# Sums of experts 1 to 6 turned back by VectorE and a scratch in memory, weight loads three chunks further ahead, gathers two experts ahead of use

## The chip, the core and the metric

The kernel runs on one core of one Trainium2 chip. The metric is the device time of one execution in microseconds (us). Engines have the names of the profile: PE is TensorE, DVE is VectorE, ACT is ScalarE, POOL is GpSimd, SP is SyncE, which here only issues DMAs.

## The reference

Retention (attention with a decay in place of the softmax) over 8 sequences of 576 tokens and 8 heads makes a row of 512 features for each of 4608 tokens. A mixture of experts follows: a token whose skip score is positive goes to one of 8 experts, and the expert's output, times its gate weight, is added to the row.

```python
ret = scores * Dmat[None, :, :, :]
x = np.matmul(ret, v).transpose(0, 2, 1, 3).reshape(B * S, H * D)      # 4608 x 512
do_compute = x @ w_skip > 0
e_idx = np.argmax(xc @ w_gate, axis=1)                                  # xc = x[do_compute]
for e in range(E):
    h = np.maximum(xc[mask] @ w1[e], 0.0)                               # 512 -> 1024
    y[mask] = gate_w[mask, None] * (h @ w2[e])                          # 1024 -> 512
out[do_compute] = xc + y
```

## The kernel before, in words

The first 160 us compute the retention, write every row to `out` in memory and rank the tokens by expert. The change lies in the rest, the experts. They are numbered 0 to 7 here, as in the code (the words "experts two to seven" count from one and mean 1 to 6), and taken in falling order of their counts. Expert e holds CAPS[e] = 368, 344, 332, 308, 304, 286, 278, 276 slots: two full blocks of 128, and a rest of 20 to 112, which is packed with the rests of other experts into a third block.

**Steps.** The 1024 hidden features are 8 chunks of 128. In step (e, f) PE computes `up` of chunk f (12 matmuls into `ph`, three for each of the four parts of the 512 inputs), then `down` of the chunk before it (12 matmuls which add to four PSUM banks `py_0` to `py_3`, each 128 output features by all slots of the expert, three matmuls a bank, one bank after the other). So the last `down` of expert e, of chunk 7, stands between `up` of chunks 0 and 1 of expert e+1, and the first `down` of expert e+1, which overwrites the four banks, stands behind `up` of chunk 1. Of the two halves of a step's place in the program, place 0 lies behind its `up`, place 1 behind its `down`.

**Precision.** Every f32 operand is split into a high part and a low rest. Of the weights ACT writes `whi` and DVE writes `wlo` from the loaded chunk `w` (4 buffers; 6 of each half). Of the hidden values ACT writes `hhi` (with the ReLU) and DVE `hlo` (lines 457 and 458), both before `down` of that chunk can run.

**Way in and out.** POOL gathers an expert's rows from `out` (`xg`, indirect DMA). SP writes them to a scratch in memory and reads them back in four pieces, a DVE transpose of 32 by 32 blocks (line 1026) turns them, ACT and DVE split them (`xhi`, `xlo`). For the way out `evacuate` copies the four banks to `yT` and `yR` (the rest), alternating ACT and DVE by bank; in the next expert's steps 1 and 2 PE turns each of the two blocks by four transposes (line 1000) and DVE's line 980 makes `rs` = gate times sum plus the old row, which POOL scatters to `out`. Expert 0 is computed with tokens on the partitions and needs no turn.

**Order.** PE runs its instructions in the order of the code. On the other engines a scheduler lays out each queue when the program is built, by its own estimate of when operands are ready; the chip then runs each queue as it was laid out. The call `split_raw` asks for the splits of the chunks that were loaded, five chunks ahead of their use (`AHEAD`).

Of the kernel before, what the change touches and what calls it, by code (L numbers as in the profile page):

```python
# [23 lines left out]
P = 128  # L24
# [9 lines left out]
NBLK = 3  # L34
# [16 lines left out]
AHEAD = 5  # L51
GROUPS = (8, 8, 8, 4, 4, 4)
# [31 lines left out]
def kernel(  # L84
# [90 lines left out]
    def by_chunk(x):  # L175
        return x.rearrange("t (p c) -> t c p", c=NCC)

# [755 lines left out]
    def down(e, f, ks, py, h, w):  # L933
        if e == 0:
            w2 = [p[:, 1].rearrange("p c i -> p (c i)") for p in w]
            for k, n in ks:
                three(py[k][:n], [([p[:, k * P : k * P + n] for p in h], w2)], f == 0, f == NFC - 1)
        else:
            m = CAPS[e]
            for c in range(NCC):  # L940
                three(py[c][:, :m], [([p[:, 1, c, :] for p in w], [p[:, :m] for p in h])], f == 0, f == NFC - 1)
# [5 lines left out]
    def evacuate(e, py):  # L947
        if e == 0:
            return py
        (q, at), n = PLACE[e], CAPS[e] - FULL  # L950
        if q not in yR:
            yR[q] = mp.tile([P, NCC, P], F32, tag="yR", name=f"yR_{q}")
            if at:
                nc.gpsimd.memset(yR[q][:, :, :at], 0.0)
        rest = yR[q]
        if e == NE - 1:
            rest = yR[e] = mp.tile([P, NCC, n], F32, tag="yE", name=f"yR_{e}", bufs=1)
        yT = mp.tile([P, NCC, FULL], F32, tag="yT", name=f"yT_{e}", bufs=1)
        copies = [nc.scalar.copy, nc.vector.tensor_copy]
        for c in range(NCC):  # L960
            copies[c % 2](yT[:, c, :], py[c][:, :FULL])
            if e < NE - 1:
                copies[c % 2](rest[:, c, at : at + n], py[c][:, FULL : FULL + n])
        if e == NE - 1:
            for c in range(NCC):
                nc.scalar.copy(rest[:, c, :], py[c][:, FULL : FULL + n])
        return yT

    def finish_rest(y, n, xr, scale, idx, tag):
        yn = bank(tag, f"yn_{y.name}", 2 if tag == "ph" else 1)  # L970
        for c in range(NCC):
            nc.tensor.transpose(yn[:n, c * P : (c + 1) * P], y[:, c, :n], ident)
        put(yn, n, scale[:n], xr[:n], idx[:n], f"rs_{y.name}")
# [19 lines left out]
    def finish(e, y, xg, ks, tags=("pt", "m")):  # L993
        for k, n in ks:
            if e == 0:
                yn = y[k]
            else:
                yn = bank(tags[k % len(tags)], f"yn_{e}_{k}", 2 if tags[k % len(tags)] == "ph" else 1)
                for c in range(NCC):
                    nc.tensor.transpose(yn[:n, c * P : (c + 1) * P], y[:, c, k * P : k * P + n], ident)  # L1000
# [22 lines left out]

    def turn_pieces(name):
# [6 lines left out]
    def gather_next(e, xg):  # L1031

        xg[e] = mp.tile([P, NBLK - 1, DM], F32, tag="xg", name=f"xg_{e}", bufs=3)
# [27 lines left out]
    def experts(acts):  # L1061
# [43 lines left out]
        at(NE - 1, 4, 0, lambda: tc.keep_in_program_order(nc.gpsimd.drain()))  # L1105
        for e in range(2, NE):
            at(e - 1, 0, 0, lambda e=e: gather_next(e, xg))
# [3 lines left out]
            for k, (name, rows) in enumerate(hops):  # L1111
                at(e - 1, 2 + k // 2, k % 2, lambda name=name, rows=rows: hop_out(name, rows()))
                at(e - 1, 3 + k // 2, k % 2, lambda name=name: hop_in(name))
        for n in range(len(steps) + 1):
# [3 lines left out]
            if cur:  # L1118
                e, f, ks = cur
                i = chunks.index((e, f))  # L1120
                for c in chunks[i : i + AHEAD + 1]:
                    if c not in wq and c not in raw and c[0] < len(regs):
                        raw[c] = load_w(*c, regs)
                if ks is not late and n > 3:
                    split_raw(1 if i == NCUT else len(raw))
# [27 lines left out]
            elif last:  # L1153
# [9 lines left out]
                if f == NFC - 1:  # L1163
                    y = evacuate(e, py[e])
                    if e + 1 < NE:
                        ks = blocks(e)[:-1] if e else blocks(e)
                        for k, where in zip(ks, ((1, 1), (2, 0), (2, 1))):
                            at(e + 1, *where, finish, e, y, xg[e], [k])
# [142 lines left out]
```

## Time and profile before

| | us |
|---|---|
| three runs | 404.70, 404.83, 405.85 (median 404.83) |
| profiled execution, its own time | 407.06 |
| its span (first to last instruction) | 405.4 |
| PE busy, share of the span | 380.5, 94% |
| DVE busy | 279.8, 69% |
| ACT busy | 184.0, 45% |
| mean granted clock of PE, of full speed | 0.992 |

The profiled execution has 1.7 us around its span and lies 2.2 us above the median of the three runs. Expert 1's first `up` starts at 199.73 us, and the last matmul of expert 7 at 396.16 us. A busy PE is not PE at its peak, since its matmuls overlap and their ends are modelled; the distance between two starts is what a matmul takes of PE's time. On DVE and ACT, too, an instruction may start some hundredths before the one ahead of it ends.

### The profile page before, as it was taken

To read this page: it belongs to the slowest core of one execution; us is meant where nothing else is said; L and a number is where in the kernel's file an instruction comes from. 1 tells how busy PE (TensorE), PEld (TensorE's weight loads), DVE (VectorE), ACT (ScalarE), POOL (GpSimd) and SP (SyncE) were. 2 spreads that over 40 slices of the span, in tenths; PEclk is the share of its full clock that TensorE was granted. 3 is DMA by queue.
4 is the path that set the end of the run, shared out by engine and by line. 5 is a ranking of instruction groups with operands and counts; after the bars stand their busy time and mean duration, and the time that the engine had idled before them with its cause. 6 is when DMAs were issued, how large, how long until landed. Compare 5 with 4: busy or idle time off the path is not lost. (4 is left out here: it accounts for less than half of the span.)

```text
span 405.4 us, 12478 instructions
## 1 busy us (share of the span) xinstructions
PE 380.5 (94%) x4950; PEld 345.4 (85%) x4952; DVE 279.8 (69%) x623; ACT 184.0 (45%) x367; POOL 154.1 (38%) x210
## 2 busy tenths in 40 slices
PE   7899989989999887999999999999999999999992
PEld 3677777778787775979899999999999999999992
DVE  3665686588589788977756766797768567777512
ACT  2454544445444566115544543545535546455311
POOL 4965654565475489051032024023042032200402
PEclk9999999999999899999999999999999999999998
DMA  8998999999999986236987666776776776673101
GB/s 304 352 331 306 352 303 350 321 335 308 331 348 325 352 327 185 81 86 224 311 261 251 202 203 212 235 254 233 244 218 238 227 243 226 233 259 107 66 2 56
DMA packets 39420, 99.34 MB, mean 245 GB/s; under 512 B 5678, under 2 KB 12974, under 8 KB 39358
## 3 DMA queue, kind: packets, MB, share of 16 engines
q1 hardware_dynamic: 30366, 78.66, 57.5%
q0 software_dynamic: 3232, 9.99, 7.2%
q10 hardware_dynamic: 5760, 9.85, 6.5%
q8 instruction: 40, 0.66, 0.7%
q14 instruction: 22, 0.18, 0.1%
HBM read 80.63 MB, written 18.26 MB: 244 GB/s over the span
## 5 line engine op out<-in xcount | busy, mean ns | idle before, releaser
L168 DVE TENSOR_TENSOR wlo_w<-w,whi_w 128x1024 fp32r<-128x1024 f32 x59 | 71.9, 1224 | 38.3 <-ACT whi_w L167 37.7
L167 ACT CAST whi_w<-w 128x1024 fp32r<-128x1024 f32 x59 | 61.7, 1051 | 52.2 <-PE py L449 48.6
L981 POOL DMA_INDIRECT out<-rs,sidx x17 | 21.5, 1264 | 126.3 <-DVE rs L980 118.1
L449 PE MATMUL ph<-xhi,whi_w 128*128 128x344 f32 (+6 forms) x224 | 68.4, 305 | 0.0
L449 PE MATMUL py<-hhi,whi_w 128*128 128x344 f32 (+6 forms) x224 | 68.2, 304 | 0.0
L449 PE MATMUL py<-hhi,wlo_w 128*128 128x344 f32 (+6 forms) x224 | 67.7, 302 | 0.0
L449 PE MATMUL ph<-xlo,whi_w 128*128 128x344 f32 (+6 forms) x224 | 67.7, 302 | 0.0
L449 PE MATMUL ph<-xhi,wlo_w 128*128 128x344 f32 (+6 forms) x224 | 67.7, 302 | 0.0
L449 PE MATMUL py<-hlo,whi_w 128*128 128x344 f32 (+6 forms) x224 | 67.6, 302 | 0.0
L588 POOL TENSOR_TENSOR kn<-u,tt_sb 128x512 f32<-128x512 f32 x33 | 35.0, 1060 | 46.6 <-DMA u<-qkv 19.4
L457 ACT ACTIVATE hhi<-ph 128x344 fp32r<-128x344 f32 (+8 forms) x61 | 26.0, 426 | 57.3 <-PE ph L449 57.2
L580 ACT COPY u<-psc 64x256 f32<-64x256 f32 x64 | 23.4, 366 | 58.5 <-DVE u L576 52.5
L670 PE MATMUL pxt<-u,vs 128*64 128x128 f32 (+1 forms) x576 | 49.0, 273 | 0.1
L607 POOL TENSOR_TENSOR vs<-u,tt_sb 64x256 f32<-64x256 f32 x72 | 44.8, 622 | 9.5 <-PE pxt L670 4.4
L576 DVE TENSOR_TENSOR u<-psc,mt_sb 64x256 f32<-64x256 f32 x72 | 30.3, 420 | 23.5 <-PE pxt L646 10.5
L621 PEld LDWEIGHTS ps_s<-u,kn 128*64 128x64 f32 x512 | 31.8, 139 | 12.8 <-issue 5.9
L449 PEld LDWEIGHTS ph<-xhi,whi_w 128*128 128x128 f32 x224 | 42.2, 189 | 0.1
L449 PEld LDWEIGHTS ph<-xlo,whi_w 128*128 128x128 f32 x224 | 42.2, 188 | 0.1
L449 PEld LDWEIGHTS py<-hhi,whi_w 128*128 128x128 f32 x224 | 42.2, 189 | 0.0
L449 PEld LDWEIGHTS py<-hlo,whi_w 128*128 128x128 f32 x224 | 42.2, 188 | 0.0
L449 PEld LDWEIGHTS py<-hhi,wlo_w 128*128 128x128 f32 x224 | 42.2, 188 | 0.0
L449 PEld LDWEIGHTS ph<-xhi,wlo_w 128*128 128x128 f32 x224 | 42.2, 188 | 0.0
(216 smaller groups left out, 825.0 us busy)
## 6 DMA issues: line engine op xcount, KB each, us to landing
u<-qkv SPq DMA_DIRECT2D x72, 512.0 KB, 5.9
w<-w SPq DMA_DIRECT2D x64, 512.0 KB, 4.6
out<-xn ACTq DMA_DIRECT2D x36, 256.0 KB, 5.9
hop<-xg SPq DMA_DIRECT2D x12, 256.0 KB, 4.7
xh<-hop SPq DMA_DIRECT2D x48, 64.0 KB, 2.7
hop_r<-xr SPq DMA_DIRECT2D x2, 256.0 KB, 2.7
xh_r<-hop_r SPq DMA_DIRECT2D x8, 64.0 KB, 5.0
out<-rs,sidx POOLq DMA_INDIRECT x17, 5.8
```

Source lines behind the costliest of these rows:

```text
L167: nc.scalar.copy(hi, t)
L168: nc.vector.tensor_tensor(lo, t, hi.bitcast(F32), ALU.subtract)
L449: nc.tensor.matmul(ps, x, y, start=first and n == 0, stop=last and n == 3 * len(terms) - 1)
L457: nc.scalar.activation(hi, ph, AF.Relu)
L576: nc.vector.tensor_tensor(u_t[g][h, j, :, :D], near[h, :, :D], mt_sb[h].unsqueeze(1).broadcast_to([D, NPR, D]), ALU.mult)
L580: nc.scalar.copy(u_t[g][h, j, :, D:], near[h, :, D:])
L588: nc.gpsimd.tensor_tensor(kn_t[g].rearrange("p a (j i) -> p a j i", j=2), u_t[g][:, 3].rearrange("p a (j i) -> p a j i", j=2), tt_sb[:, k ...
L607: nc.gpsimd.tensor_tensor(vs_t[g][h, j], u_t[g][h, 2, :, j * D : (j + 1) * D], tt_sb[h, TV + g % NQ // 2, :].unsqueeze(2).broadcast_to([D, ...
L621: nc.tensor.matmul(ps_s[halves[j], i % 2, a, :], kn_t[g][:, a, j * D : (j + 1) * D], u_t[g][:, 2, a, j * D : (j + 1) * D], start=i == 0 an ...
L670: nc.tensor.matmul(pxt[halves[j], a, q], vs_t[g][:, j, a, :], u_t[g][:, j, a, q], start=False, stop=a == NPR - 1, skip_group_check=True,)
L981: done = nc.gpsimd.indirect_dma_start(out=out, out_offset=bass.IndirectOffsetOnAxis(ap=idx, axis=0), in_=rs[:n], in_offset=None, bounds_ch ...
```

## The change

For experts 1 to 6 PE's transposes of the two full blocks go. `evacuate` lets DVE transpose each of the four banks in 32 by 32 blocks out of PSUM (`yp`), and leaves all copies of the rest, `yR`, to ACT. `pieces_out` writes `yp` to a scratch in memory in four DMAs of 128 KB (runs of 512 bytes), `rows_in` reads it back as rows (`yr`, one DMA of 512 KB), and `finish` takes `yr` in place of PE's result, in step 4 of the next expert. So that the pieces of 32 features lie right, the columns of `w2` are stored in another order, expert 0's `down` reads them in runs of 32, and the transposes that are left (line 981 of the new kernel) write in runs of 32.

From expert 1 on, loads of weights are issued up to 8 chunks ahead, with the same 4 buffers; the splits stay 5 ahead, and at an expert's first step (from expert 2 on) they are asked for behind the evacuation. Gathers are issued an expert earlier, with a fourth buffer of `xg`, and the hops of the gathered rows two steps earlier; POOL's drain moves from step 4 to step 6 of expert 7.

```diff
@@ -49,6 +49,7 @@
 UAHEAD = UBUFS - LAG
 VBUFS = 3
 AHEAD = 5
+LEAD = 3
 GROUPS = (8, 8, 8, 4, 4, 4)
 KONE = 2
 QD = 32
@@ -174,6 +175,9 @@
 
     def by_chunk(x):
         return x.rearrange("t (p c) -> t c p", c=NCC)
+
+    def by_piece(x):
+        return x.rearrange("t (p c i) -> t c p i", p=NQD, i=QD)
 
     def route_a(t0, n):
 
@@ -932,9 +936,10 @@
 
     def down(e, f, ks, py, h, w):
         if e == 0:
-            w2 = [p[:, 1].rearrange("p c i -> p (c i)") for p in w]
+            w2 = [p[:, 1].rearrange("f c (p i) -> f p c i", i=QD) for p in w]
             for k, n in ks:
-                three(py[k][:n], [([p[:, k * P : k * P + n] for p in h], w2)], f == 0, f == NFC - 1)
+                to = py[k][:n].rearrange("t (p c i) -> t p c i", p=NQD, i=QD)
+                three(to, [([p[:, k * P : k * P + n] for p in h], w2)], f == 0, f == NFC - 1)
         else:
             m = CAPS[e]
             for c in range(NCC):
@@ -955,12 +960,16 @@
         rest = yR[q]
         if e == NE - 1:
             rest = yR[e] = mp.tile([P, NCC, n], F32, tag="yE", name=f"yR_{e}", bufs=1)
+        if e < NE - 1:
+            yp = mp.tile([P, FULL // QD, NCC, QD], F32, tag="yp", name=f"yp_{e}", bufs=1)
+            for c in range(NCC):
+                marks["evacuated"] = nc.vector.transpose(yp[:, :, c, :], py[c][:, :FULL].rearrange("p (j t) -> p j t", t=QD))
+                nc.scalar.copy(rest[:, c, at : at + n], py[c][:, FULL : FULL + n])
+            return yp
         yT = mp.tile([P, NCC, FULL], F32, tag="yT", name=f"yT_{e}", bufs=1)
         copies = [nc.scalar.copy, nc.vector.tensor_copy]
         for c in range(NCC):
             copies[c % 2](yT[:, c, :], py[c][:, :FULL])
-            if e < NE - 1:
-                copies[c % 2](rest[:, c, at : at + n], py[c][:, FULL : FULL + n])
         if e == NE - 1:
             for c in range(NCC):
                 nc.scalar.copy(rest[:, c, :], py[c][:, FULL : FULL + n])
@@ -969,7 +978,7 @@
     def finish_rest(y, n, xr, scale, idx, tag):
         yn = bank(tag, f"yn_{y.name}", 2 if tag == "ph" else 1)
         for c in range(NCC):
-            nc.tensor.transpose(yn[:n, c * P : (c + 1) * P], y[:, c, :n], ident)
+            nc.tensor.transpose(by_piece(yn[:n])[:, c], y[:, c, :n], ident)
         put(yn, n, scale[:n], xr[:n], idx[:n], f"rs_{y.name}")
 
     def finish_pack(q):
@@ -992,12 +1001,12 @@
 
     def finish(e, y, xg, ks, tags=("pt", "m")):
         for k, n in ks:
-            if e == 0:
-                yn = y[k]
+            if e == 0 or e in yr:
+                yn = yr[e][:, k, :] if e else y[k]
             else:
                 yn = bank(tags[k % len(tags)], f"yn_{e}_{k}", 2 if tags[k % len(tags)] == "ph" else 1)
                 for c in range(NCC):
-                    nc.tensor.transpose(yn[:n, c * P : (c + 1) * P], y[:, c, k * P : k * P + n], ident)
+                    nc.tensor.transpose(by_piece(yn[:n])[:, c], y[:, c, k * P : k * P + n], ident)
             put(yn, n, gate[:n, k, e : e + 1], xg[:n, k, :], sidx[:n, k, e : e + 1], f"rs_{e}_{k}")
 
     xr, xrT, xh, hop = {}, {}, {}, {}
@@ -1020,6 +1029,20 @@
         rows = hop.pop(name).rearrange("(h t) (p c) -> p t h c", t=QD, c=P)
         for p in range(NQD):
             nc.sync.dma_start(xh[name][p * QD : (p + 1) * QD], rows[p])
+
+    def pieces_out(e, yp):
+        with tc.issue_after(marks["load"].ins):
+            hop[e] = dram.tile([FULL, DM], F32, tag="hopy", name=f"hopy_{e}")
+            rows = hop[e].rearrange("(j t) (p c) -> p t j c", t=QD, c=P)
+            for p in range(NQD):
+                nc.sync.dma_start(rows[p], yp[p * QD : (p + 1) * QD].rearrange("t j c i -> t j (c i)"))
+
+    def rows_in(e):
+        with tc.issue_after(marks["load"].ins):
+            yr[e] = mp.tile([P, FULL // P, DM], F32, tag="yr", name=f"yr_{e}", bufs=1)
+            nc.sync.dma_start(yr[e], hop.pop(e).rearrange("(k t) c -> t k c", t=P))
+
+    yr = {}
 
     def turn_pieces(name):
         xt = mp.tile([P, NCC, P], F32, tag="xt", name=f"xt_{name}")
@@ -1030,7 +1053,7 @@
 
     def gather_next(e, xg):
 
-        xg[e] = mp.tile([P, NBLK - 1, DM], F32, tag="xg", name=f"xg_{e}", bufs=3)
+        xg[e] = mp.tile([P, NBLK - 1, DM], F32, tag="xg", name=f"xg_{e}", bufs=4)
         gather(e, xg[e], blocks(e)[:-1])
         q = PLACE[e][0]
         if q not in xr:
@@ -1102,15 +1125,16 @@
         at(2, 7, 1, count_more)
         at(0, 6, 0, pack_move)
         at(0, 7, 1, lambda: behind("up", pack_ids))
-        at(NE - 1, 4, 0, lambda: tc.keep_in_program_order(nc.gpsimd.drain()))
+        at(NE - 1, 6, 0, lambda: tc.keep_in_program_order(nc.gpsimd.drain()))
         for e in range(2, NE):
-            at(e - 1, 0, 0, lambda e=e: gather_next(e, xg))
+            at(*{2: (1, 0), 3: (1, 5)}.get(e, (e - 2, 0)), 0, lambda e=e: gather_next(e, xg))
             hops = [(f"{e}_{k}", lambda e=e, k=k: xg[e][:, k, :]) for k in range(NBLK - 1)]
             if e == PACKS[PLACE[e][0]][0]:
                 hops.append((f"r{PLACE[e][0]}", lambda e=e: xr[PLACE[e][0]]))
             for k, (name, rows) in enumerate(hops):
-                at(e - 1, 2 + k // 2, k % 2, lambda name=name, rows=rows: hop_out(name, rows()))
-                at(e - 1, 3 + k // 2, k % 2, lambda name=name: hop_in(name))
+                n = (e - 1) * NFC - 2 * (e > 3) + k // 2
+                at(*divmod(n, NFC), k % 2, lambda name=name, rows=rows: hop_out(name, rows()))
+                at(*divmod(n + 1, NFC), k % 2, lambda name=name: hop_in(name))
         for n in range(len(steps) + 1):
             cur = steps[n] if n < len(steps) else None
             if n in acts:
@@ -1118,11 +1142,12 @@
             if cur:
                 e, f, ks = cur
                 i = chunks.index((e, f))
-                for c in chunks[i : i + AHEAD + 1]:
+                for c in chunks[i : i + AHEAD + 1 + (LEAD if e else 0)]:
                     if c not in wq and c not in raw and c[0] < len(regs):
                         raw[c] = load_w(*c, regs)
-                if ks is not late and n > 3:
-                    split_raw(1 if i == NCUT else len(raw))
+                due = sum(c in chunks[: i + AHEAD + 1] for c in raw)
+                if ks is not late and n > 3 and (f or e < 2):
+                    split_raw(1 if i == NCUT else due)
                 if (e, f) not in hs:
                     tg, nb = (f"_{f}", 1) if e == 0 and f < NCUT else ("", 3)
                     hs[e, f] = [
@@ -1162,10 +1187,17 @@
                 down(e, f, ks, py[e], hs[e, f], wq[e, f])
                 if f == NFC - 1:
                     y = evacuate(e, py[e])
+                    if 0 < e < NE - 1:
+                        with tc.issue_after(marks["evacuated"].ins):
+                            split_raw(due)
                     if e + 1 < NE:
-                        ks = blocks(e)[:-1] if e else blocks(e)
-                        for k, where in zip(ks, ((1, 1), (2, 0), (2, 1))):
-                            at(e + 1, *where, finish, e, y, xg[e], [k])
+                        if e:
+                            at(e + 1, 0, 1, pieces_out, e, y)
+                            at(e + 1, 2, 0, rows_in, e)
+                            at(e + 1, 4, 1, lambda e=e: behind("up", finish, e, None, xg[e], blocks(e)[:-1]))
+                        else:
+                            for k, where in zip(blocks(e), ((1, 1), (2, 0), (2, 1))):
+                                at(e + 1, *where, finish, e, y, xg[e], [k])
                         if e and PACKS[PLACE[e][0]][-1] == e:
                             at(e + 1, 2, 1, finish_pack, PLACE[e][0])
                     else:
@@ -1292,7 +1324,9 @@
     wg = np.zeros((P, NCC, WP), f)
     wg[:, :, :NW] = w9
     w1 = moe_w1.reshape(NE, NCC, P, NFC, P).transpose(0, 3, 2, 1, 4).reshape(NE, NFC, P, DM)
-    w2 = moe_w2.reshape(NE, NFC, P, NCC, P).swapaxes(3, 4).reshape(NE, NFC, P, DM)
+    place = np.arange(DM).reshape(P, NCC).T.ravel()
+    there = np.argsort(place)[np.arange(DM).reshape(NQD, NCC, QD).swapaxes(0, 1).ravel()]
+    w2 = moe_w2.reshape(NE, NFC, P, DM)[..., there]
     w = np.ascontiguousarray(np.concatenate([w1, w2], axis=3))
     ins = {"qkv": qkv, "mtab": mtab, "gtab": gtab, "ttab": ttab, "wg": wg, "w": w}
```

The following shows where DVE's and ACT's queues differ. DVE at the boundary from expert 6 to expert 7, before; `hlo_0` and `hlo_1` are of expert 7's chunks 0 and 1, `py_` of expert 6, `wlo_w_5` of a chunk of expert 7.

```order
L168 TENSOR_TENSOR wlo_w_4_5830_5833<-w_4_5830,whi_w_4_5830_5832 128x1024
L458 SCALAR_TENSOR_TENSOR hlo_0_5872<-ph_0_0_5873,hhi_0_5871 128x276
L961 COPY yT_5900<-py_1_5594 128x256
L963 COPY yR_5213<-py_1_5594 128x22
L961 COPY yT_5900<-py_3_5596 128x256
L963 COPY yR_5213<-py_3_5596 128x22
L168 TENSOR_TENSOR wlo_w_5_5865_5868<-w_5_5865,whi_w_5_5865_5867 128x1024
L458 SCALAR_TENSOR_TENSOR hlo_1_5916<-ph_1_0_5917,hhi_1_5915 128x276
```

The same place of the changed kernel; `rs` and `yr` are of expert 5, the `wlo` of chunks 1 to 4 of expert 7.

```order
L169 TENSOR_TENSOR wlo_w_1_5583_5699<-w_1_5583,whi_w_1_5583_5698 128x1024
L462 SCALAR_TENSOR_TENSOR hlo_0_5857<-ph_0_0_5858,hhi_0_5856 128x276
L966 STREAM_TRANSPOSE yp_5885<-py_0_5606 128x8x32
L169 TENSOR_TENSOR wlo_w_2_5622_5748<-w_2_5622,whi_w_2_5622_5747 128x1024
L989 SCALAR_TENSOR_TENSOR rs_0_5735<-yr_5645,both,xg_4509 128x512
L989 SCALAR_TENSOR_TENSOR rs_1_5740<-yr_5645,both,xg_4509 128x512
L966 STREAM_TRANSPOSE yp_5885<-py_1_5607 128x8x32
L966 STREAM_TRANSPOSE yp_5885<-py_2_5608 128x8x32
L169 TENSOR_TENSOR wlo_w_3_5659_5787<-w_3_5659,whi_w_3_5659_5786 128x1024
L966 STREAM_TRANSPOSE yp_5885<-py_3_5609 128x8x32
L169 TENSOR_TENSOR wlo_w_4_5696_5824<-w_4_5696,whi_w_4_5696_5823 128x1024
L462 SCALAR_TENSOR_TENSOR hlo_1_5908<-ph_1_0_5909,hhi_1_5907 128x276
```

Between `hlo_0` and `hlo_1` stood two copies of 256 columns, two of 22 and one weight split; now four transposes, three weight splits and two `rs` stand there, and the last bank is read behind all but one of them.

DVE at the boundary from expert 5 to expert 6 of the changed kernel (`rs` of expert 4; the queue before had the pattern of the first piece above).

```order
L966 STREAM_TRANSPOSE yp_5565<-py_0_5270 128x8x32
L169 TENSOR_TENSOR wlo_w_2_5286_5412<-w_2_5286,whi_w_2_5286_5411 128x1024
L989 SCALAR_TENSOR_TENSOR rs_0_5399<-yr_5309,both,xg_4091 128x512
L989 SCALAR_TENSOR_TENSOR rs_1_5404<-yr_5309,both,xg_4091 128x512
L462 SCALAR_TENSOR_TENSOR hlo_0_5537<-ph_0_0_5538,hhi_0_5536 128x278
L966 STREAM_TRANSPOSE yp_5565<-py_1_5271 128x8x32
L169 TENSOR_TENSOR wlo_w_3_5323_5451<-w_3_5323,whi_w_3_5323_5450 128x1024
L966 STREAM_TRANSPOSE yp_5565<-py_2_5272 128x8x32
L169 TENSOR_TENSOR wlo_w_4_5360_5492<-w_4_5360,whi_w_4_5360_5491 128x1024
L966 STREAM_TRANSPOSE yp_5565<-py_3_5273 128x8x32
L169 TENSOR_TENSOR wlo_w_5_5409_5575<-w_5_5409,whi_w_5_5409_5574 128x1024
L462 SCALAR_TENSOR_TENSOR hlo_1_5590<-ph_1_0_5591,hhi_1_5589 128x278
```

Here the first transpose, a split and both `rs` even stand ahead of `hlo_0`, and the other three transposes have a split between each two.

ACT at the same boundary, before and then now.

```order
L457 ACTIVATE hhi_0_5525<-ph_0_0_5527 128x278
L961 COPY yT_5561<-py_0_5247 128x256
L963 COPY yR_5213<-py_0_5247 128x30
L961 COPY yT_5561<-py_2_5249 128x256
L167 CAST whi_w_5_5519_5521<-w_5_5519 128x1024
L963 COPY yR_5213<-py_2_5249 128x30
L457 ACTIVATE hhi_1_5576<-ph_1_0_5578 128x278
```

```order
L461 ACTIVATE hhi_0_5536<-ph_0_0_5538 128x278
L967 COPY yR_5227<-py_0_5270 128x30
L168 CAST whi_w_3_5323_5450<-w_3_5323 128x1024
L461 ACTIVATE hhi_1_5589<-ph_1_0_5591 128x278
L967 COPY yR_5227<-py_1_5271 128x30
L168 CAST whi_w_4_5360_5491<-w_4_5360 128x1024
L967 COPY yR_5227<-py_2_5272 128x30
L168 CAST whi_w_5_5409_5574<-w_5_5409 128x1024
L967 COPY yR_5227<-py_3_5273 128x30
```

The four `yR` copies, which with the transposes set the banks free, now lie one behind each of three weight casts, three of them behind `hhi_1`, which itself waits for `up` of chunk 1.

## Rows read from the trace of the kernel before

**Rows 1.** Waits of PE from 170 us on (total, times, longest).
```profile
PE py L449 <- DVE hlo L458: 0.7, 1, 0.7
```

**Rows 2.** Length, busy us of PE, PEld, DVE, ACT, POOL; clock; DMA share.
```profile
337.00:364.00 27.00, 27.00 (x211) 27.00 (x210) 19.48 (x29) 14.70 (x24) 2.91 (x3) 1.00 0.69 232
```

**Rows 3.** PE's turns back of sums (min/median/max ns, first, last start).
```profile
L1000 PE MATMUL yn<-ident,yT x56: 270/272/329, 237.5 to 397.5; 128*128 128x128 f32 x56
```

**Rows 4.** Timeline of PE around one turn (start us, us, instruction, count).
```profile
349.52 0.30 PE L449 MATMUL py<-hhi,wlo_w 128*128 128x278 f32 x1
349.65 0.60 PE L1000 MATMUL yn<-ident,yT 128*128 128x128 f32 x4
350.01 0.37 PE L449 MATMUL ph<-xhi,whi_w 128*128 128x278 f32 x1
350.22 0.29 PE L449 MATMUL ph<-xlo,whi_w 128*128 128x278 f32 x1
```

**Rows 5.** DVE by line, 227 to 400 us (busy us, mean ns | idle).
```profile
L168 DVE TENSOR_TENSOR wlo_w<-w,whi_w 128x1024 fp32r<-128x1024 f32 x45 | 55.1, 1224 | 29.3 <-ACT whi_w L167 28.7 <-PE ph L449 0.3
...
L1026 DVE STREAM_TRANSPOSE xt<-xh 128x512 f32<-128x512 f32 x10 | 11.0, 1101 | 0.0
L980 DVE SCALAR_TENSOR_TENSOR rs<-yn,both,xg 128x512 f32<-128x512 f32 x14 | 10.4, 747 | 5.7 <-PE yn L1000 5.6
L173 DVE TENSOR_TENSOR xlo<-xt,xhi 128x512 fp32r<-128x512 f32 x10 | 6.8, 685 | 0.7 <-ACT xhi L172 0.7
L961 DVE COPY yT<-py 128x256 f32<-128x256 f32 x14 | 5.9, 421 | 2.9 <-PE py L449 2.8
```

**Rows 6.** ACT by line, the same stretch.
```profile
L167 ACT CAST whi_w<-w 128x1024 fp32r<-128x1024 f32 x45 | 47.3, 1051 | 42.6 <-PE py L449 41.5 <-DMA xh<-hop 1.1
...
L963 ACT COPY yR<-py 128x88 f32<-128x88 f32 (+5 forms) x12 | 2.5, 208 | 0.0
```

**Rows 7.** Timeline of PE, boundary from expert 5 to 6.
```profile
345.24 0.30 PE L449 MATMUL py<-hhi,wlo_w 128*128 128x286 f32 x1
...
348.10 0.29 PE L449 MATMUL py<-hhi,whi_w 128*128 128x278 f32 x1
...
349.27 0.29 PE L449 MATMUL py<-hhi,whi_w 128*128 128x278 f32 x1
```

**Rows 8.** Timeline of DVE, the same boundary.
```profile
345.71 0.44 DVE L458 SCALAR_TENSOR_TENSOR hlo<-ph,hhi 128x278 fp32r<-128x278 f32 x1
346.07 0.42 DVE L961 COPY yT<-py 128x256 f32<-128x256 f32 x1
```

**Rows 9.** Timeline of ACT, the same boundary.
```profile
346.64 1.05 ACT L167 CAST whi_w<-w 128x1024 fp32r<-128x1024 f32 x1
347.60 0.18 ACT L963 COPY yR<-py 128x30 f32<-128x30 f32 x1
```

**Rows 10.** Timeline of ACT, boundary from expert 6 to 7.
```profile
370.90 0.40 ACT L457 ACTIVATE hhi<-ph 128x276 fp32r<-128x276 f32 x1 [0.67 <-PE ph L449]
```

**Rows 11.** Timeline of PE, the same boundary.
```profile
374.85 0.29 PE L449 MATMUL py<-hhi,whi_w 128*128 128x276 f32 x1
```

**Rows 12.** Timeline of ACT, boundary from expert 3 to 4.
```profile
287.87 0.29 ACT L172 CAST xhi<-xt_r 128x120 fp32r<-128x120 f32 x1
```

**Rows 13.** Timeline of PE, the same boundary.
```profile
294.84 0.30 PE L449 MATMUL py<-hhi,whi_w 128*128 128x304 f32 x1
```

**Rows 14.** Timeline of ACT, boundary from expert 4 to 5.
```profile
315.94 0.26 ACT L172 CAST xhi<-xt_r 128x88 fp32r<-128x88 f32 x1
```

**Rows 15.** Timeline of PE, the same boundary.
```profile
322.67 0.29 PE L449 MATMUL py<-hhi,whi_w 128*128 128x286 f32 x1
```

**Rows 16.** Timeline of ACT at the end of expert 7.
```profile
396.95 0.17 ACT L966 COPY yR<-py 128x20 f32<-128x20 f32 x1 [0.31 <-DVE yT L961]
```

**Rows 17.** DMA issues (count, KB each, median us to landing).
```profile
w<-w SPq DMA_DIRECT2D x64, 512.0 KB, 4.6
```

**Rows 18.** PE by line, 170 to 210 us: transposes that read every fourth element.
```profile
L930 PE MATMUL pt<-ident,xg 128*128 128x128 f32 x12 | 2.2, 279 | 0.0
```

## The prediction

> **What bounds the kernel now.** I read the waits of PE from the first expert on, then the busy time of all engines in windows of one expert, then the timeline of PE, DVE and ACT at each boundary between two experts. The first says that PE waits for nothing worth a name in 236 us: its largest entry is one wait of 0.7 us [rows 1]. The second says the same from the other side: over an expert PE is busy 27.00 of 27.00 us at a granted clock of 1.00, while DVE is busy 19.48 and ACT 14.70 [rows 2]. So in the stretch that the change touches, time goes only with work that leaves PE's queue, and comes only with waits that enter it. DVE and ACT have about a quarter and a half of each expert idle, but an idle share is no promise for the few us at a boundary, and there the timelines have to be followed instruction by instruction.
>
> **What PE loses.** PE turns sums by 56 transposes, four to a block [rows 3]. Of the 14 blocks, the 12 of experts 1 to 6 go, the two of expert 7 stay. A group of four starts at 349.65, just behind a matmul that started at 349.52, and the second matmul behind it starts at 350.22 [rows 4]; the rows between show the group and one more matmul. From 349.65 to 350.22 are 0.57 us, less the 0.13 us that one matmul takes (349.52 to 349.65): 0.44, say 0.43 us. 12 x 0.43 = 5.2 us go.
>
> **What the boundary asks for.** Behind the last `down` of an expert PE has `up` of the next expert's chunk 1 and then its first `down`, which overwrites the four banks. Bank c is needed three matmuls after bank c-1: at the boundary from 5 to 6 the last `down` of expert 5 starts at 345.24, the first of expert 6 at 348.10, and bank 3 is needed at 349.27 [rows 7]. Before, DVE had 0.42 us of copy for a bank and started on them at 346.07, right behind `hlo_0` [rows 8]. Now each bank needs a transpose on DVE and then the `yR` copy on ACT; where both read one bank, ACT's copy starts behind DVE's read [rows 16]. The queues run in order: the `yR` copy at 347.60 reads a bank that was full since 345.5 and starts only when the weight cast ahead of it is over [rows 9]. So what stands between the transposes in the new queues is on the path, however early its operands were ready.
>
> **Prices.** A transpose of 256 columns out of PSUM isn't in this trace. Half of the 512-column transpose from SBUF, which takes 1.10 us, is 0.55; a copy of the same bank takes 0.42 [rows 5], the lower bound; the upper is 0.62, if the transpose has a fixed part of 0.15 us (1.10 less 0.15, halved, plus 0.15; the fixed part is an estimate from the copy of 30 columns, which takes 0.18 [rows 9]). I take 0.55, since it comes from the same instruction. `rs` took 0.75 with one operand in PSUM; now all three lie in SBUF, and the nearest row is `xlo` with 0.69; `wlo` takes 1.22 [rows 5]. Starts on DVE follow about 0.08 closer than the durations (345.71 + 0.44 against 346.07 [rows 8]), so a queue advances by 0.47 for a transpose, 0.61 for `rs`, 1.15 for `wlo`, 0.36 for `hlo`.
>
> [...]
>
> **Boundary 5 to 6.** The order of DVE shown above: the last `down` ends at 345.54; transpose 0 from 345.57, `wlo_2` from 346.04, two `rs` from 347.19, `hlo_0` from 348.41, transpose 1 from 348.77, `wlo_3` from 349.24, transpose 2 from 350.39, `wlo_4` from 350.86, transpose 3 from 352.01 to 352.56, and ACT's copy of the rest behind it to 352.77. Bank 3 was needed at 349.27: 3.5 us of wait. (`hlo_0`, needed at 348.10, is late as well, but bank 3 is later.)
>
> **Boundary 6 to 7.** `hhi_0` starts at 370.90 [rows 10]; behind it ACT casts `whi_2` until 372.32, and `wlo_2`, which needs it, starts at 372.35 on DVE. Then two `rs`, transposes 1 and 2, `wlo_3` (from 375.66), transpose 3 to 377.36, the rest to 377.55. Needed at 374.85 [rows 11]: 2.7 us.
>
> **Boundaries 3 to 4 and 4 to 5.** By the new order a cast of the packed block (`xhi`, at 287.87 [rows 12] and 315.94 [rows 14]) stands ahead of `whi_2`, which thus ends at 289.15 and 317.20. On DVE follow `wlo_2`, two `rs`, `hlo_0`, transpose 0, `wlo_3`, transpose 1, `wlo_4`, transpose 2. Transpose 2 ends at 295.72 and 323.79 and its rest at 295.96 and 324.0; bank 2 is needed at 294.84 [rows 13] and 322.67 [rows 15]: 1.1 and 1.35 us. At 1 to 2 and 2 to 3 the splits stand behind the transposes in the order, or no `rs` is due yet, and I find no wait.
>
> Together 3.5 + 2.7 + 1.1 + 1.35 = 8.65 us come, 5.2 go: **+3.45 us**. With the profiled execution's own 407.06 that is 410.5; the median of the runs lies 2.2 below it, so 404.83 + 3.45 = 408.3.
>
> **The ends.** 13 transposes stand on these four paths (4 + 3 + 3 + 3). At 0.42 each is 0.13 shorter: waits 6.95, net +1.75, 406.6. At 0.62 they add 0.9, and eight `rs` at 0.75 another 0.5: net +4.85, 409.7. Were the transposes free, 5 to 6 would still keep 2.0 us by ACT alone (`hhi_1` ends at about 348.8, and two casts of 1.05 us [rows 6] stand ahead of the last `yR`), and 6 to 7 would keep 2.7 - 1.4 = 1.3: net -1.9, 402.9.
>
> **What else is added.** `down` of expert 0 reads its weights in runs of 32. PE's transposes that read every fourth element take 279 ns against 272 [rows 18, 3]; 72 matmuls would pay at most 72 x 7 ns = 0.5 us, and nothing if a run of 32 counts as straight; I take nothing, being nearer to no stride, and keep the 0.5 in the range. Each of the six experts sends 512 KB out and the same back. At a DMA share of 0.69 for 232 GB/s [rows 2] the queues could carry 336 GB/s, so 1.05 MB are 3.1 us of all of them; a load lands in 4.6 us [rows 17] and its splits, by the new order, come three steps later than before but still two steps ahead of use. A step is (374.85 - 349.27) / 8 = 3.2 us [rows 7, 11]. Four buffers give a load 4 x 3.2 = 12.8 us from one release to the next need; 4.6 + 3.1 + two splits of 2.3 us are 10.0, so it stays hidden by 2.8 us, and costs 3.1 where that cover goes. The gathers and POOL's drain feed only `xg` and the scatters, which are several steps ahead of any use; nothing for them, from nothing to 0.5 us. Expert 7's end is the same work as before.
>
> **Rivals.** (a) *The gain stands.* The transposes and casts find the banks free in time, and PE keeps the 5.2 us: 399.6, and up to 402.9 with transposes at nothing. For it speaks only DVE's quarter of idle time [rows 2]; against it the orders, in which two or three weight splits lie between the transposes, and rows 9, in which a queue doesn't pass a waiting or long instruction. It counts as faster only where the waits come to 4.0 us or less, 4.65 below my sum, that is, where DVE is more than a whole split ahead of where I put it at each of the four boundaries. (b) *They cancel.* Transposes near the copy's 0.42 and splits faster by a tenth when DVE doesn't wait: each of the twelve splits on the four paths 0.1 shorter is another 1.2 off the 6.95: waits of 5.75, net +0.55, 405.4. For it speaks that `wlo`'s mean of 1.22 comes from a kernel in which other engines were at the same memory; against it the 1.10 of the transpose. (c) *Weights late too.* SP issues a load only when the split behind which it waits has been done, and the new DMAs of `yp` and `yr` stand between loads on its queue; where one of the six places loses its cover PE waits a further 3.1 us: 411.4. For it speaks the share of 0.69, against it the 2.8 us of cover. The point from which it decides is a load that lands more than 12.8 - 2.3 = 10.5 us after its release.
>
> **How the numbers follow.** Forecast 0.60, 406.6 to 409.7 by itself; (a) 0.12; (b) 0.15; (c) 0.13. What a measurement of this kernel can tell from no change is about 0.3%, 1.2 us: 403.6 to 406.0 counts as the same, which is (b). Slower is the forecast and (c), 0.73; faster is (a), 0.12. The range of 403.6 to 411.5 leaves out (a) and half of (c).
>
> **What the profile after would show.** Turns of `yn` are 8 in place of 56. PE waits for `py`, released by DVE's transpose or ACT's `yR`, at the four boundaries, longest at 5 to 6 (about 3.5 us), 2.7 at 6 to 7, and by 1 to 1.4 at the two others; none at 1 to 2 and 2 to 3. The transposes take 0.42 to 0.62 us. PE's waits for `wlo` and `whi` stay near zero; if they don't, (c) is at work. The prediction is wrong if PE's waits for `py` together stay under 5 us, or if a boundary's wait ends with another releaser.

## The result

The changed kernel takes 410.96 us (median of 12 runs, 407.27 to 414.97) against 404.87 for the kernel before: the ratio is 1.0124, 95% interval 1.0085 to 1.0162, so 1.2% slower, about 5.0 us. Two of the twelve runs (414.09 and 414.97) count as slow and are left out of the ratio. The profiled execution took 412.98 us, with a span of 411.3.

Of the 56 turns of `yn` on PE 8 are left. What came in their place stands in the waits of PE, from 170 us on (who waits for whom: total us, times, longest), which answer to [rows 1]:

```profile
PE py L453 <- ACT yR L967: 5.0, 7, 1.2
PE py L453 <- DVE hlo L462: 1.1, 2, 0.6
```

DVE at the boundary from expert 5 to 6 (start us, us, instruction, count; in brackets the idle time before it and who ended it):

```profile
341.87 0.45 DVE L966 STREAM_TRANSPOSE yp<-py 128x256 f32<-128x256 f32 x1 [0.73 <-PE py L453]
342.24 1.18 DVE L169 TENSOR_TENSOR wlo_w<-w,whi_w 128x1024 fp32r<-128x1024 f32 x1
343.35 1.40 DVE L989 SCALAR_TENSOR_TENSOR rs<-yr,both,xg 128x512 f32<-128x512 f32 x2
344.67 0.44 DVE L462 SCALAR_TENSOR_TENSOR hlo<-ph,hhi 128x278 fp32r<-128x278 f32 x1
345.02 0.44 DVE L966 STREAM_TRANSPOSE yp<-py 128x256 f32<-128x256 f32 x1
345.39 1.18 DVE L169 TENSOR_TENSOR wlo_w<-w,whi_w 128x1024 fp32r<-128x1024 f32 x1
346.49 0.44 DVE L966 STREAM_TRANSPOSE yp<-py 128x256 f32<-128x256 f32 x1
346.86 1.18 DVE L169 TENSOR_TENSOR wlo_w<-w,whi_w 128x1024 fp32r<-128x1024 f32 x1
347.96 0.44 DVE L966 STREAM_TRANSPOSE yp<-py 128x256 f32<-128x256 f32 x1
```

DVE doesn't idle once from the first transpose to the last, and ends the fourth at 348.40. PE at the same place, which answers to [rows 7]:

```profile
344.39 0.29 PE L453 MATMUL py<-hhi,whi_w 128*128 128x278 f32 x1
345.17 0.40 PE L453 MATMUL py<-hlo,whi_w 128*128 128x278 f32 x1 [0.48 <-DVE hlo L462]
...
347.20 0.40 PE L453 MATMUL py<-hhi,whi_w 128*128 128x278 f32 x1 [0.81 <-ACT yR L967]
...
348.67 0.60 PE L453 MATMUL py<-hhi,whi_w 128*128 128x278 f32 x1 [0.82 <-ACT yR L967]
349.06 0.44 PE L453 MATMUL py<-hlo,whi_w 128*128 128x278 f32 x1
...
349.53 0.43 PE L453 MATMUL ph<-xhi,whi_w 128*128 128x278 f32 x1
349.76 0.43 PE L453 MATMUL ph<-xlo,whi_w 128*128 128x278 f32 x1
...
354.62 0.36 PE L453 MATMUL py<-hlo,whi_w 128*128 128x278 f32 x1
354.82 0.30 PE L453 MATMUL py<-hhi,wlo_w 128*128 128x278 f32 x1
354.96 0.29 PE L453 MATMUL ph<-xhi,whi_w 128*128 128x278 f32 x1
```

Bank 3 is overwritten from 348.67 on, just behind its `yR`. Then something that no row of before shows: from there to 354.82 matmuls of 278 columns start 0.23 us apart in place of 0.13. The windows (length, busy us of PE, PEld, DVE, ACT, POOL; clock; DMA share) of this and of the next boundary name it:

```profile
345.00:350.00 5.00, 3.16 (x14) 2.49 (x15) 4.86 (x8) 2.97 (x7) 2.15 (x2) 0.79 0.94 341
350.00:355.00 5.00, 5.00 (x24) 5.00 (x24) 1.67 (x2) 0.99 (x2) 0.00 (x0) 0.52 0.63 179
355.00:360.00 5.00, 5.00 (x41) 5.00 (x41) 1.58 (x2) 1.60 (x3) 0.00 (x0) 1.00 0.96 301
...
375.00:380.00 5.00, 3.04 (x17) 2.59 (x16) 5.00 (x9) 4.22 (x8) 2.75 (x2) 0.87 0.67 211
380.00:385.00 5.00, 5.00 (x35) 5.00 (x34) 3.21 (x5) 1.86 (x3) 0.00 (x0) 0.79 0.70 209
```

PE's granted clock falls to half near the end of the waits: it is 0.50 in every window of 1 us from 348 to 354, and again from 379 to 382. Worked out from these mean values it stays there for 6.9 us the first time, (0.21 + 0.48) x 5 / 0.5, and for 3.4 us the second. Before it was 1.00 at the first of these places [rows 2] and at the second:

```profile
375.00:380.00 5.00, 5.00 (x44) 5.00 (x43) 3.21 (x5) 2.24 (x3) 2.52 (x2) 1.00 0.15 56
380.00:385.00 5.00, 5.00 (x42) 5.00 (x42) 2.36 (x4) 1.06 (x3) 1.88 (x2) 1.00 0.22 78
```

PE is busy through all of 350 to 355, and the clock is back at 1.00 from 355 to 360; so the fall stands in the middle of a busy kernel, behind waits of 0.5 to 1.2 us each.

The starts of each expert's first `up` give a sharper account than the time of an execution, since that start itself lies anywhere from 196.9 to 201.8 us in the profiles here. Lengths in us from one expert's first `up` to the next one's, and for expert 7 to the start of the last `down`:

| expert | 1 | 2 | 3 | 4 | 5 | 6 | 7 | all |
|---|---|---|---|---|---|---|---|---|
| before | 30.43 | 30.56 | 28.25 | 28.07 | 26.38 | 25.70 | 27.04 | 196.43 |
| changed | 30.47 | 29.67 | 27.38 | 28.19 | 26.66 | 30.73 | 30.21 | 203.31 |
| e5 below | 30.48 | 29.67 | 27.38 | 27.15 | 25.48 | 24.79 | 26.17 | 191.12 |

Experts 2 and 3 gain 0.88 each. Experts 4 to 7, whose starts hold the four boundaries, lie 1.04, 1.18, 5.94 and 4.04 above e5, which has the same PE work and no waits there: 12.2 us.

### The profile page after: what moved, and what is told of

It reads as the page before. It is cut to its first block, busy times and chain, and to the rows that moved or that the text cites. A ratio compares the mean times of both kernels' runs of the same rounds, so it can differ in the third digit from the quotient of the medians.

```text
span 411.3 us, 12392 instructions
## 1 busy us (share of the span) xinstructions
PE 379.9 (92%) x4904; PEld 342.9 (83%) x4904; DVE 280.3 (68%) x623; ACT 180.4 (44%) x367; POOL 151.5 (37%) x210
## 5 line engine op out<-in xcount | busy, mean ns | idle before, releaser
L453 PE MATMUL py<-hhi,whi_w 128*128 128x344 f32 (+6 forms) x224 | 69.4, 310 | 5.0 <-ACT yR L967 5.0
L453 PE MATMUL py<-hlo,whi_w 128*128 128x344 f32 (+6 forms) x224 | 68.5, 306 | 0.5 <-DVE hlo L462 0.5
L453 PE MATMUL ph<-xlo,whi_w 128*128 128x344 f32 (+6 forms) x224 | 68.9, 307 | 0.0
L453 PE MATMUL ph<-xhi,wlo_w 128*128 128x344 f32 (+6 forms) x224 | 68.8, 307 | 0.0
L462 DVE SCALAR_TENSOR_TENSOR hlo<-ph,hhi 128x344 fp32r<-128x344 f32 (+8 forms) x61 | 28.9, 473 | 29.2 <-ACT hhi L461 28.6
L674 PE MATMUL pxt<-u,vs 128*64 128x128 f32 (+1 forms) x576 | 47.8, 269 | 0.0
L453 PEld LDWEIGHTS py<-hlo,whi_w 128*128 128x128 f32 x224 | 43.1, 192 | 0.7 <-DVE hlo L462 0.7
L453 PEld LDWEIGHTS ph<-xhi,whi_w 128*128 128x128 f32 x224 | 43.4, 194 | 0.1
L453 PEld LDWEIGHTS ph<-xlo,whi_w 128*128 128x128 f32 x224 | 43.3, 193 | 0.1
L453 PEld LDWEIGHTS ph<-xhi,wlo_w 128*128 128x128 f32 x224 | 43.4, 194 | 0.0
```

Source lines behind the costliest of these rows:

```text
L453: nc.tensor.matmul(ps, x, y, start=first and n == 0, stop=last and n == 3 * len(terms) - 1)
L462: marks["up"] = nc.vector.scalar_tensor_tensor(lo, ph, 0.0, hi.bitcast(F32), ALU.max, ALU.subtract)
L674: nc.tensor.matmul(pxt[halves[j], a, q], vs_t[g][:, j, a, :], u_t[g][:, j, a, q], start=False, stop=a == NPR - 1, skip_group_check=True,)
```

## The experiments

Their ratios are to runs of the kernel before on the same chip. In the edits `...` stands for lines left out.

**e1, another queue.** My theory was the order; a rival was that the turn costs time by itself.

```diff
-                nc.sync.dma_start(rows[p], yp[p * QD : (p + 1) * QD].rearrange("t j c i -> t j (c i)"))
+                nc.gpsimd.dma_start(rows[p], yp[p * QD : (p + 1) * QD].rearrange("t j c i -> t j (c i)"))
-            nc.sync.dma_start(yr[e], hop.pop(e).rearrange("(k t) c -> t k c", t=P))
+            nc.gpsimd.dma_start(yr[e], hop.pop(e).rearrange("(k t) c -> t k c", t=P))
```

> The changed kernel with the DMAs of yp and yr issued by POOL in place of SP; nothing else is edited, and no work is left out. In the program's order this puts the four transposes of a boundary side by side again, with the splits of chunks 2 to 4 and both rs ahead of the boundary. Theory A (what costs is the order in which splits and rs stand between the transposes, and the clock that falls behind the waits): PE's waits at the boundaries go from 6.1 us to under 1, the granted clock stays 1.00 over the experts, and the 5.2 us of removed transposes remain: 399.7 us, 398.5 to 401. Rival B (the transposes out of PSUM, the 6 MB of extra traffic or the stored order of w2 cost the time themselves): it stays above 405. Rival C (POOL's own issues become late for the scatters): 402 to 406, with waits for rs or yr.

407.80 us, ratio 1.0056 (1.0024 to 1.0087). By its time alone this would be rival B, above 405; the waits say otherwise. PE no longer waits for a bank, but 5.1 us for `hlo`, and the reason stands on DVE:

```profile
274.55 1.08 DVE L1049 STREAM_TRANSPOSE xt<-xh 128x512 f32<-128x512 f32 x1
279.15 1.41 DVE L989 SCALAR_TENSOR_TENSOR rs<-yr,both,xg 128x512 f32<-128x512 f32 x2 [3.52 <-DMA yr<-hopy]
...
282.22 0.47 DVE L462 SCALAR_TENSOR_TENSOR hlo<-ph,hhi 128x308 fp32r<-128x308 f32 x1
```

`rs` waits for `yr`, and `hlo` of the next chunk is queued behind it. Nobody is in a hurry for `rs`; it costs only because of its place. The waits are those of rival C, though the time lies above its 406: behind the longest of them, 2.2 us, the clock fell here too, and expert 3 is 3.94 us longer than in e5.

```profile
284.00:287.00 3.00, 3.00 (x13) 3.00 (x13) 3.00 (x5) 1.86 (x4) 0.10 (x1) 0.50 0.86 229
```

**e2, the turn without the loads and gathers.** Gathers, hops and drain go back to their places, the buffers of gathered rows to three.

```diff
-LEAD = 3
+LEAD = 0
...
-            at(*{2: (1, 0), 3: (1, 5)}.get(e, (e - 2, 0)), 0, lambda e=e: gather_next(e, xg))
+            at(e - 1, 0, 0, lambda e=e: gather_next(e, xg))
...
-                n = (e - 1) * NFC - 2 * (e > 3) + k // 2
+                n = (e - 1) * NFC + 2 + k // 2
```

(So in the change the hops of experts 4 to 7 stand four steps earlier, not two; of the gathers, expert 2's stays and expert 3's moves by three steps only.)

> The changed kernel with loads issued no further ahead than before and gathers, hops and drain where they were; the turn by DVE and the scratch stays. Theory A (the new DMAs on SP's queue set the order, not the loads or gathers): the order still has two or three splits between the transposes of the last three boundaries, and waits of 8 to 10 us are expected in all, with a fallen clock at two of them: 409 to 413 us. Rival D (loads three chunks further ahead and earlier gathers make the splits late): 399.5 to 401.

411.05 us, 1.0143 (1.009 to 1.0197). Splits stand between the transposes at the last four boundaries again, and PE waits for the banks, so the loads further ahead didn't cause it. The experts take 200.82 us, 9.7 above e5, all of it waits: the clock stayed at 1.00 there, against what I expected. But not all of it is the order:

```profile
PE py L453 <- ACT yR L967: 3.9, 7, 0.8
PE ph L453 <- ACT xhi L173: 2.3, 2, 1.1
PE ph L453 <- DVE xlo L174: 0.7, 2, 0.3
```

The last 3.0 us are for the gathered rows of experts 6 and 7, which the changed kernel has in time. For the turn on SP's queue, too, the earlier gathers and hops are worth something.

**e3, the loads and gathers without the turn.**

```diff
-                for c in chunks[i : i + AHEAD + 1]:
+                for c in chunks[i : i + AHEAD + 1 + (LEAD if e else 0)]:
...
-            at(e - 1, 0, 0, lambda e=e: gather_next(e, xg))
+            at(*{2: (1, 0), 3: (1, 5)}.get(e, (e - 2, 0)), 0, lambda e=e: gather_next(e, xg))
```

> The kernel before with only the loads three chunks further ahead, the gathers, hops and drain moved, and a fourth buffer for gathered rows. Theory A: nothing of it is on PE's path, 404.9 us within 1. Rival D: the splits come late here as well, 407 or more.

404.76 us, 0.9997 (0.9966 to 1.0028); the seven lengths are those of before to 0.01 us. By themselves they do nothing.

**e4, waits alone.** The kernel before, and DVE made late at two boundaries.

```diff
...
+                with tc.issue_after(marks["up"].ins):
+                    for k in range(1 if c == 1 else 2):
+                        marks["up"] = nc.vector.tensor_tensor(pad, pad, pad, ALU.subtract)
...
                 copies[1](yT[:, c, :], py[c][:, :FULL])
```

> The kernel before with three subtractions of 128 x 1024 on a tile of their own added to DVE between the copies of the banks at the boundaries 5 to 6 and 6 to 7, so that PE waits there once each for about 2.8 us; the rest is as before. Theory A (a wait of PE is what brings the clock down): the waits add 5.7 us, and the granted clock falls behind at least one of them as it did in the changed kernel, for another 1.5 to 4 us: 412 to 415 us. Rival E (the clock fell by something else in the changed kernel, its traffic or its transposes): clock 1.00 over all experts, 410.6 us.

414.57 us, 1.0216 (1.0175 to 1.0258). The clock falls in a kernel with none of the change's traffic or transposes, but behind the second wait only (each is 2.7 us long in the profile's waits):

```profile
350.00:353.00 3.00, 0.37 (x3) 0.14 (x2) 2.94 (x5) 0.00 (x0) 0.00 (x0) 1.00 0.59 165
353.00:356.00 3.00, 2.91 (x24) 2.94 (x25) 1.81 (x2) 1.32 (x2) 0.78 (x1) 1.00 0.55 177
...
378.00:381.00 3.00, 0.89 (x7) 0.67 (x6) 3.00 (x5) 0.18 (x1) 0.00 (x0) 1.00 0.00 0
381.00:384.00 3.00, 2.37 (x14) 2.40 (x15) 1.76 (x5) 1.05 (x1) 0.25 (x1) 0.77 0.02 5
384.00:387.00 3.00, 3.00 (x19) 3.00 (x18) 1.72 (x3) 0.40 (x1) 1.48 (x1) 0.66 0.23 87
```

Expert 6 became 2.93 us longer and expert 7 4.57: the same wait, and 1.64 us of slow matmuls on top. Behind one wait of 2.7 us the clock came down (0.66 from 384 to 387), behind another it didn't (1.00 from 353 to 356).

**e5, e1 with `rs` later.**

```diff
-                            at(e + 1, 4, 1, lambda e=e: behind("up", finish, e, None, xg[e], blocks(e)[:-1]))
+                            at(e + 1, 6 if e < NE - 2 else 4, 1, lambda e=e: behind("up", finish, e, None, xg[e], blocks(e)[:-1]))
```

> e1 with one more edit: finish, which asks for the two rs, stands in step 6 of the next expert in place of step 4 (expert 6's stays in step 4 of expert 7); no work is left out. In e1 yr landed 5.4 to 8.3 us after its issue and hlo of chunk 5 stood behind the rs that waited for it. Theory A (the removed transposes are worth 5.2 us once nothing waits): no wait of PE over 0.7 us in the experts, clock 1.00 there, the stretch from expert 1's first up to the last matmul 191.4 us against 196.4 before, 399.9 us, 399 to 401. Rival B (the turn by DVE and memory itself costs PE time, by traffic or by the stored order of w2): 403 or more. Rival C (rs late in step 6 as well): waits for hlo again, 402 to 406.

402.12 us, 0.992 (0.9894 to 0.9947). The four transposes of a boundary stand side by side, and the experts take 191.12 us, 5.3 below before, with one wait left, of 0.6 us, which before has as well [rows 1]:

```profile
340.14 1.43 DVE L966 STREAM_TRANSPOSE yp<-py 128x256 f32<-128x256 f32 x4
...
PE py L453 <- DVE hlo L462: 0.6, 1, 0.6
```

The 6 MB of traffic, the transposes out of PSUM and the stored order of `w2` cost PE nothing in experts 1 to 7: 196.43 less the forecast's 5.2 is 191.2. But behind the last matmul 11.27 us follow in place of 9.24, which is where 2 of the 5.3 us went.

**e6, ACT's queue in place of POOL's.** As e1, with the other engine's name; against e1, the line of `yr` (that of `yp` alike):

```diff
-            nc.gpsimd.dma_start(yr[e], hop.pop(e).rearrange("(k t) c -> t k c", t=P))
+            nc.scalar.dma_start(yr[e], hop.pop(e).rearrange("(k t) c -> t k c", t=P))
```

> The changed kernel with the DMAs of yp and yr issued by ACT in place of SP; nothing else is edited. The transposes of a boundary stand side by side, but ACT issues four DMAs and casts one weight chunk ahead of hhi of chunk 1. Theory A (the waits of each queue's order add up, whatever they wait for): one wait of 0.8 to 1.1 us for hlo of chunk 1 at each of six boundaries, together 6 us against 5.2 gained: 405.7 us, 404.5 to 407, with a clock that falls behind few of these short waits or none. Rival F (ACT has room to issue them): 400.

419.28 us, 1.0289 (1.0225 to 1.0353): a clear miss. Four issues alone take 3.11 us of ACT, and the next weight cast and `hhi` stand behind them. PE's two waits at this boundary end before `yr` is issued:

```profile
265.73 3.11 ACTq L1038 DMA_DIRECT2D hopy<-yp  x4
268.88 1.05 ACT L168 CAST whi_w<-w 128x1024 fp32r<-128x1024 f32 x1 [2.93 <-DMA hopy<-yp]
269.83 0.74 ACT L461 ACTIVATE hhi<-ph 128x308 fp32r<-128x308 f32 x2
274.45 0.39 ACTq L1043 DMA_DIRECT2D yr<-hopy  x1
...
270.31 0.41 PE L453 MATMUL py<-hhi,whi_w 128*128 128x308 f32 x1 [0.87 <-ACT hhi L461]
271.63 0.41 PE L453 MATMUL py<-hlo,whi_w 128*128 128x308 f32 x1 [0.91 <-DVE hlo L462]
```

In all PE waits 11.8 us, 5.7 of them for `hhi`, which I hadn't counted, and the clock was at 0.83 in four windows of 10 us.

**e7, e5 without the loads and gathers.** The edits of e2, made on e5.

```diff
-LEAD = 3
+LEAD = 0
...
-            at(*{2: (1, 0), 3: (1, 5)}.get(e, (e - 2, 0)), 0, lambda e=e: gather_next(e, xg))
+            at(e - 1, 0, 0, lambda e=e: gather_next(e, xg))
...
```

> e5 without the loads three chunks further ahead and with the gathers, hops and drain where they were before: the turn by DVE and the scratch on POOL's queue alone. Theory A (loads and gathers are off PE's path): as e5 or 0.5 us more, 400 to 401.5. Rival G (without earlier gathers the rows of the next expert come late, since POOL's queue now holds the DMAs of yp and yr as well): 403 or more, with waits for xhi or xlo.

429.98 us, 1.0575 (1.0507 to 1.0643): rival G, and by far. POOL now scatters, sends and gathers in one queue, and gathers that were not issued ahead reached the next expert late: at one place DVE idled 8.31 us for their rows:

```profile
315.80 1.08 DVE L1049 STREAM_TRANSPOSE xt<-xh 128x512 f32<-128x512 f32 x1 [8.31 <-DMA xh<-hop]
```

So the part of the change that does nothing by itself (e3) is what the repaired turn stands on. This row speaks for the gathers; the weight loads were put back with them, and what they are worth alone isn't shown.

**e8, the order put back.** e5 with three splits asked for between the four transposes at two boundaries.

```diff
...
+                if e in (5, 6) and c:
+                    with tc.issue_after(marks["evacuated"].ins):
+                        split(1)
+                    with tc.issue_after(marks["wlo"].ins), tc.issue_after(marks["whi"].ins):
+                        marks["evacuated"] = nc.vector.transpose(yp[:, :, c, :], py[c][:, :FULL].rearrange("p (j t) -> p j t", t=QD))
...
```

> e5 with the order put back at two boundaries only: at 5 to 6 and 6 to 7 the splits wlo of chunks 3, 4 and 5 stand between the four transposes on DVE, as in the changed kernel; the DMAs stay on POOL's queue, and the weight casts on ACT and both rs stay ahead of the boundary. The work is the same, only its place on DVE differs. Theory A (the order between the transposes makes the waits): two waits at each of the two boundaries, 0.8 and 1.1 us, 3.9 us in all; without a fall of the clock 4 us above e5, with falls behind them up to 4 more; the stretch from expert 1's first up to the last matmul 195 to 199 us against 191.1. Rival H (the queue that carries the DMAs made the difference, not the order): as e5, 191.1.

405.77 us, 0.9987 (0.9954 to 1.002). The experts take 195.18 us: expert 6 is 1.97 and expert 7 2.08 longer than in e5, the rest equal to 0.01, and the clock stays at 1.00. The same work in another order costs 4.06 us. The ratios say about the same: they lie 0.7 to 0.9% above those of e5 and of its second round (e10), 2.7 to 3.8 us.

```profile
PE py L453 <- ACT yR L971: 2.9, 4, 0.8
```

**e9, `rs` one step earlier than in e5.**

```diff
-                            at(e + 1, 6 if e < NE - 2 else 4, 1, lambda e=e: behind("up", finish, e, None, xg[e], blocks(e)[:-1]))
+                            at(e + 1, 5 if e < NE - 2 else 4, 1, lambda e=e: behind("up", finish, e, None, xg[e], blocks(e)[:-1]))
```

> e5 with finish in step 5 in place of step 6. In e1 the latest rs was 2.2 us behind what hlo of chunk 5 needed, and one step is 3.2 us. Theory A: no waits, the stretch of the experts 191.1 us as in e5, and the same time within 1 us. Rival C (yr lands too late for step 5): waits for hlo of chunk 6, above e5 by the wait. The profile also tells whether the 11.3 us behind the last matmul in e5, against 9.2 before, belong to that kernel or to that execution.

406.21 us, 1.0002 (0.9964 to 1.004); the experts take 197.76. Rival C again:

```profile
336.99 0.75 DVE L989 SCALAR_TENSOR_TENSOR rs<-yr,both,xg 128x512 f32<-128x512 f32 x1 [3.78 <-DMA yr<-hopy]
```

PE waits 3.5 us for the `hlo` behind it, the clock fell there (0.57 from 341 to 345), and one step too early gives back the whole gain.

**e10, e5 a second time.**

> e5 once more, word for word the same kernel, for the 2 us between the 5.3 us that its experts gained and the 3.2 us that its time gained. If they belong to the kernel's end, the stretch behind the last matmul is 11 us again in this profile and the time 402 us again; if they belong to that execution, the stretch is 9.0 to 9.4 us as in most kernels here, and the time 400 us. The stretch of the experts is 191.1 us in both cases.

401.30 us, 0.9894 (0.985 to 0.9938), the experts 191.10, the end 11.17: the 2 us belong to that kernel's end. The changed kernel has 10.65 there, the others that share e5's step 11.05 (e7) and 10.81 (e8), e1 and e9 9.4. The last transposes, `rs` and scatters are the same, instruction by instruction. Most of the difference is the landing of the last scatter (the last number: us from issue to landing), before and e10:

```profile
out<-rs_yR,sidx POOLq DMA_INDIRECT x1, 2.1
out<-rs_yR,sidx POOLq DMA_INDIRECT x1, 3.9
```

It is 3.9 in the changed kernel as well and 3.5 in e8, but 2.0 to 2.1 in e1, e2, e3, e4 and e6 (e5, e7 and e9 have no record of it). Why it lands later stays open.

## Why the prediction was right, and what it lacked

- *PE's loss, 12 x 0.43 = 5.2 us.* 5.3 in e5. Right.
- *The order decides, not the share of idle time.* Right: e8 makes the waits by order alone, e5 takes them away with the same work.
- *The waits, 8.65 us.* At the boundaries 3 to 4, 4 to 5, 5 to 6 and 6 to 7 I put 1.1, 1.35, 3.5 and 2.7; the lengths give 1.04, 1.18 and, without the slow matmuls, 3.1 and 2.4: 7.7. The mis-sized term is the transpose: 0.44 us (median of 24), not 0.55. I halved the 1.10 of a transpose of 512 columns from SBUF; the copy's 0.42, the lower bound, which gave 6.95, was nearly right. Why the two transposes differ by the column no run shows. With 0.44 the thirteen transposes would bring my sum to 7.2; the 0.5 from there to 7.7 I can't assign.
- *Nothing for runs of 32, traffic, loads and POOL.* e3 and e5 bear it out, as long as the gathers go ahead (e2, e7). Of the runs of 32 the timelines tell: in expert 0's last `down` eight starts take 1.85 us before and 1.88 now, 0.2 to 0.3 us for all 72, and so more than nothing but inside the 0.5.

```profile
197.88 0.39 PE L449 MATMUL py<-wlo_w,hhi 128*128 128x512 f32 x1
...
199.73 0.32 PE L449 MATMUL ph<-xhi,whi_w 128*128 128x344 f32 x1
```

```profile
195.46 0.40 PE L453 MATMUL py<-wlo_w,hhi 128*128 128x512 f32 x1
...
197.34 0.32 PE L453 MATMUL ph<-xhi,whi_w 128*128 128x344 f32 x1
```

- *Nothing for the end of expert 7, "the same work as before".* The same work, but 10.65 us in place of 9.24 in the two profiles: 1.4 us that I hadn't counted.
- *The missing term.* I had PE lose its waits and nothing more. From 348.67 to 354.82 stand 26 starts in 6.15 us, where 26 x 0.13 = 3.4 would do; at 6 to 7, 15 starts in 3.54 us in place of 1.95. That is 2.8 + 1.6 = 4.4 us. 7.7 + 4.4 - 5.2 = 6.9, which is the 203.31 less 196.43. With 1.4 at the end, and expert 1's first `up` 2.4 us earlier, these are the 5.9 us between the two profiled executions.

So the forecast of +3.45 us for about +5.0 is a gain and waits of about the right size, and a clock and an end that I didn't price. That the measured 410.96 lies in my range is in part luck: the forecast by itself reached only to 409.7, the rest up to 411.5 was there for late weights, which didn't come, and transposes priced too dear made up for a part of the clock. The clock goes with the spread, loosely: in runs with a mean clock of 0.991 or more the changed kernel took 407.3 to 409.2 us, in two with 0.981 412.3 and 413.0, in those between 407.8 to 411.4. Without a fall the sum of gain and waits is 7.7 - 5.2 = +2.5. Rival (a) needs waits that don't come; e5 shows what it takes. Rival (b) had the right transpose, but the splits stayed at 1.18 us where it wanted a tenth less. Rival (c), late weights, didn't happen: PE waits for no `whi` or `wlo`.

Where the bad order came from is shown as far as this: with the DMAs of `yp` and `yr` on SP the splits stand late in the built order, with or without the further loads (e2), on POOL or ACT they don't. That the scheduler took the loads behind them on SP's queue for late is my reading of it.

The best version here is e5: the change with its new DMAs on POOL's queue and `finish` in step 6, 0.8 to 1.1% faster than before.

## What to carry to other kernels

When work leaves a saturated engine, print the new order of the engines that take it over, and walk the few microseconds where the saturated one needs their result; an idle quarter of DVE was no help while three weight splits lay between four short reads, which cost 4.06 us at two boundaries of e8. An instruction without a deadline (`rs`) must stand behind the one that has one, or its own wait becomes the deadline's: in e1 `rs` waited 3.52 us for `yr`, and PE 2.2 us for the `hlo` behind it. Where PE is the bound, price a wait at its length and keep room for slower matmuls behind it: a fall of the clock cost 1.6 us in the changed kernel's second case and in e4, and 2.8 us in the first, 0.56 to 0.9 of the waits ahead of it.

## What the runs showed that I had not expected

The granted clock of PE fell to half (0.50 from 348 to 354 in the changed kernel, and from 284 to 287 in e1) in the middle of a busy stretch, behind waits of PE: in the changed kernel twice, for 2.8 and 1.6 us of lost time, in e1 and e9 once, in e6 four times (behind two waits of 0.9 us, for one), in e4 behind one of two waits of the same length, in e2 and e8 behind none. What separates them these runs don't tell. Issuing DMAs wasn't free for the issuer: 3.11 us for four on ACT. That POOL's queue is the slower one for `yr` isn't shown: its landings on record take 5.4 and 8.3 us in e1 and 4.5 to 6.6 in e10, and the only one on record on SP 4.8.
